# Gated linear attention and an eight-expert layer in one kernel: other places for the expert searches, the weight splits and one table update

## The chip, the cores and the metric

The kernel runs on one core of a Trainium2 chip. The metric is the device time of one launch in microseconds (us); lower is better. Inside the core, TensorE (PE; PEld is its weight load), VectorE (DVE), ScalarE (ACT) and GpSimd (POOL) work side by side, each through its own instructions strictly in the order in which they were written. SyncE (SP) and, for a few transfers, ACT and POOL issue DMAs.

## What is computed

Two stages follow each other. The first is a gated linear recurrence for 4 batches of 8 heads (768 steps, head size 48). The second routes the resulting 3072 rows of 384 numbers to 8 experts, 384 rows each, and applies each expert's two-layer network. Routing is greedy: all (row, expert) scores are taken from the highest down, and a row goes to the first expert that still has room.

```python
for t in range(S):                                   # first stage
    state = alpha[:, :, t, :, None] * state + einsum('bhd,bhe->bhde', k[:, :, t], v[:, :, t])
    y[:, :, t] = einsum('bhd,bhde->bhe', q[:, :, t], state)
x = y.transpose(0, 2, 1, 3).reshape(3072, 384)

order = argsort(-(x @ w_gate).flatten())             # second stage
for idx in order:
    tok, e = idx // 8, idx % 8
    if assigned[tok] >= 0 or counts[e] >= 384: continue
    assigned[tok] = e; counts[e] += 1
for e in range(8):
    out[assigned == e] = relu(x[assigned == e] @ w1[e]) @ w2[e]
```

## The kernel before, in words

**First stage (to about 130 us of the span).** 24 steps of scans, small matmuls and transposes make the rows x, which go to a DRAM tile `x_dram`, and the router's logits `L` (128 partitions x 24 columns x 8 experts). The change doesn't touch it.

**Routing as eight searches.** Instead of sorting, the kernel finds the expert that fills up first, settles its rows, and repeats. Each search compares a 32-bit key in five digits, "levels" 0 to 4:

- `table` (L595, instruction L547): DVE compares every row's digit with all values of a ramp and writes a table `cmp`, 3072 columns wide in levels 0 and 1, 1536 or 1560 in levels 2 to 4.
- `counts` (L598): PE sums the table in 24 small matmuls.
- `reached` (L603): DVE compares the counts with the room left, giving `g` (L605).
- `flags` (L585): one PE matmul spreads `g`, and DVE reduces it to `k` (L588). `next_digit` makes `nd` (L592) and the next level's table follows.

After level 4 come `find` (which expert, and the issue of the first half of its weights' DMAs), `offsets`, `places`, `one_hot` (DVE writes `hot`, 3072 columns, L682, and then `rhs`, L684), `index` (24 PE matmuls over `hot`, L691) and `gather` (DVE turns the result into `idx`, L696; POOL issues three indirect DMAs that fetch the expert's rows `xr`, L698; SP then issues the second half of the weights). `best_left` takes the filled expert out of `L` (L720), finds each row's best remaining logit `m_c` (L721), and makes new digits; `new_choice` and `left` finish that.

**Expert networks on PE.** Each fp32 product is made of three matmuls with split operands: weights as `whi` (ACT copies, `split_hi`, L771 and L772) and `wlo` (POOL subtractions of 128x384, `split_lo`, L780; 16 for an expert, n = 0 to 15, two for each of eight column groups q), rows as `xh` (ACT, L801) and `xl` (DVE, L806). `ffn1` of group q (f1(q), 9 matmuls, L818) leaves `h` in PSUM. ACT makes `hh` of it (L823), then DVE `hl` (L824), and `ffn2` of group q (f2(q), 9 matmuls, L838) uses both. An expert has 144 such product matmuls in the order f1(0), f1(1), f1(2), f2(0), f1(3), f2(1), ... f1(7), f2(5), f2(6), f2(7). `hh` and `hl` of a group are written into their engines' order together with the last matmul of that group.

**What sets the order.** From L956 on a plan gives every step of the searches a position counted in product matmuls: `at(pos, step)` puts a step ahead of product `pos`. The loop at L963 plans round i from a position `base`. Round i starts with `index` results of expert i, fetches expert i's rows, splits its weights, and runs the search for expert i+1, all between products of expert i-1 and the first products of expert i. A round lasts `end` products; `offs` are the positions of the five levels, `hi` and `lo` those of the weight splits, and the triples after `rows` those of the row transposes. Rounds 1 to 5 have a five-level search; round 6 has a short one, round 7 none. What stands ahead of round 1 (round 0) is written out by hand (L921 to L960).

**POOL and DVE.** `BEHIND` (L15) gives for each n which DVE instruction of the running search the POOL subtraction n has to wait for (a dependency made by hand, L780 to L786): entries 0 to 4 are the five tables. For the last expert another rule holds.

Of the kernel before, what the change touches and what calls it, by code (L numbers as in the profile page):

```python
# [11 lines left out]
F16 = mybir.dt.float16  # L12
ROUTE_AHEAD = 3
LAST_BLOCKS = 2
BEHIND = (0, 0, 0, 1, 1, 2, 2, 3, 3, 4, 4, 4, 4, 4, 4, 4)  # L15
FREE_LAST = 4
WARM_UP = 10
Y_IN_LEVEL = (None, 11, 8, 8, 8)
# [8 lines left out]
OP = mybir.AluOpType  # L27
# [3 lines left out]
def gla_moe_kernel(ctx, tc, q, k, v, alpha, w_gate, w1, w2, out):  # L31
    nc = tc.nc
# [9 lines left out]
    E = w_gate.shape[1]  # L42
# [20 lines left out]
    BIGNEG = -3.0e38  # L63
# [455 lines left out]
    def col(x, n=NU):  # L519
        return x[:, None, :].to_broadcast([128, n, x.shape[-1]])  # L520
# [157 lines left out]
    def one_hot(i):  # L678
        hot = st["hot"] = rw.tile([128, NW, T, U], F16, name="hot", bufs=1)
        rhs = st["rhs"] = rw.tile([128, NU, NB], F16, name="rhs")  # L680
        for a, js in enumerate(halves(i)):
            x = nc.vector.tensor_tensor(words(hot, T, js), keyed(st["wb"], T, js), each(iota, T, js), op=OP.is_equal)  # L682
            if a == 0:
                nc.vector.tensor_tensor(rhs, st["bk"], row(cst_c, NB), op=OP.mult)  # L684
        if i == E - 1:
            compared[i] = [None] * FREE_LAST + [x]

    def index(i):
        ix = psx.tile([128, NB], F32, name="xt")
# [27 lines left out]

    def best_left(i):
        es, v = st["es"], st["v"]
        nc.vector.scalar_tensor_tensor(L, col(cl_c), BIGNEG, L, op0=OP.mult, op1=OP.add)  # L720
        nc.vector.tensor_reduce(m_c, L, axis=X, op=OP.max)  # L721
        nc.vector.scalar_tensor_tensor(sel_c, v, float(CAP), qe_c, op0=OP.is_le, op1=OP.mult)
        val = st["val"] = rw.tile([128, NU, E], BF, name="val")
        if i + 2 < E:
            sg = rw.tile([128, NU], I32, name="sg")
            nc.vector.tensor_scalar(sg, m_c.bitcast(I32), 31, -2 ** 31, op0=OP.arith_shift_right,
                                    op1=OP.bitwise_or)
            nc.vector.scalar_tensor_tensor(asg, sel_c, es, asg, op0=OP.mult, op1=OP.add)  # L728
            nc.vector.tensor_tensor(key_c, m_c.bitcast(I32), sg, op=OP.bitwise_xor)
            nc.vector.tensor_tensor(val, L, row(m_c, E), op=OP.is_equal)  # L730
            nc.vector.tensor_tensor(di_c, key_c[:, None, :].to_broadcast([128, nb, NU]), shifts,
                                    op=OP.logical_shift_right)
            nc.vector.tensor_tensor(di_c, di_c, masks, op=OP.bitwise_and)
            top = st["top"] = rw.tile([128, NU], BF, name="top")
            nc.vector.tensor_scalar(top, di_c[:, 0], 1.0, None, op0=OP.add)
            st["d"] = top
        else:
            nc.vector.scalar_tensor_tensor(asg, sel_c, es, asg, op0=OP.mult, op1=OP.add)
            nc.vector.tensor_tensor(val, L, row(m_c, E), op=OP.is_equal)
# [35 lines left out]
    def split_lo(i, n):  # L775
        q, h = divmod(n, 2)
        if (i, q) not in CH:
            return False
        hi, lo, x = CH[i, q]
        y = nc.gpsimd.tensor_sub(lo[:, h], x[h], hi[:, h])  # L780
        if i + 1 in compared:
            after = compared[i + 1][BEHIND[n] if i + 2 < E else min(n, FREE_LAST)]
            if after is not None:
                tc.add_manual_dep(y.ins, after.ins.name,
                                  mybir.DependencyInfo(mybir.DependencyClass.Sync, mybir.DependencyReason.DATA),
                                  reason="weights split while the search reads one table at a time")  # L786
# [96 lines left out]
    def at(pos, fn, *args):  # L883
        plan.append((pos, len(plan), fn, args))
# [76 lines left out]
        at(p, split_lo, 0, n)  # L961
    base = 90
    for i in range(1, E):  # L963
        offs = dict(enumerate((36, 51, 65, 79, 93)))
        end = 140 if i == 1 else 144
        renewed(base, i) if i < E - 1 else at(base, gather, i)
        if i < E - 1:
            at(base + 9, new_choice, i)
        if i < E - 2:
            at(base + 14, table, i + 1, 0)  # L970
            at(base + 14, left, i)
        for b, p in enumerate((25, 34, 41) if i < E - 1 else (45, 60, 75)):
            at(base + p, rows, i, b)
        if i < E - 2:
            levels(base, i + 1, offs, {0: (0, 1), 1: (2,)})
            found(base + offs[4] + 3, i + 1, end - offs[4] - 3)
        else:
            for b, p in enumerate((29, 38, 45) if i < E - 1 else (49, 64, 79)):
                at(base + p, rows_lo, i, b)
        if i == E - 2:  # L980
            at(base + 12, find_last, i + 1)
# [3 lines left out]
            end = 58  # L985
            at(base + end, index, i + 1)
        if i < E - 2:
            hi = (24, 32, 50, 64, 86, 98, 108, 118)
            lo = (26, 26, 32, 55, 55, 71, 71, 87, 87, 103, 103, 103, 108, 108, 118, 118)
        elif i == E - 2:  # L990
            hi = (24, 32, 50, 64, 80, 96, 106, 118)
            lo = (26, 27, 32, 33, 50, 51, 64, 65, 80, 81, 96, 97, 106, 107, 118, 119)
        else:
            hi = [80 + 18 * q for q in range(5)] + [160, 170, 206]
            lo = [x for p in hi for x in (p, p + 1)]
# [70 lines left out]
```

## Time and profile before

| | |
|---|---|
| three timed runs | 425.99, 426.4 (median), 431.81 us |
| the profiled execution | 424.76 us, its span 423.1 us |
| busy share of the span | PE 93%, PEld 82%, DVE 68%, POOL 63%, ACT 46% |
| granted TensorE clock | 0.978 over the span |
| first `index` matmul (L691) of experts 0 to 7 | 151.35, 183.53, 216.58, 250.24, 284.01, 317.76, 351.52, 363.85 us |

Times in the trace are counted from the start of the span. The `index` matmuls make good milestones: round i runs from the i-th of them to the next, so rounds 2 to 5 take 33.7 to 33.8 us each and round 1 takes 33.05 us. A row of the timeline has the start, the duration, the engine, the source line, the operation, what it writes and reads, and in brackets how long the engine sat idle before it and what ended that. In the rows the shown duration of a matmul overlaps with the next one: products start 0.17 us apart, though each is shown with 0.33 us. So a wait of PE is the idle time in brackets plus about 0.17 us.

### The profile page before, as it was taken

How to read it: one execution, taken by the hardware profiler on the slowest of the kernel's cores; microseconds unless marked ns; L12 is line 12 of the kernel's file. 1: busy time of each engine (PE TensorE's matmuls, PEld its weight loads, DVE VectorE, ACT ScalarE, POOL GpSimd, SP SyncE). 2: the span in 40 equal slices, each digit the busy share in tenths (PEclk: the TensorE clock that was granted, in tenths of full speed). 3: DMA queues.
4: the chain of work that ended last, by engine and by line, in shares of the span. 5: the costliest groups of instructions: out<-in, count | busy, mean ns of one | idle time of the engine just before them, and what ended most of it. 6: DMA issues, size and time to landing. Idle time of an engine off the chain costs nothing.

```text
span 423.1 us, 10874 instructions
## 1 busy us (share of the span) xinstructions
PE 394.1 (93%) x4151; PEld 345.5 (82%) x4151; DVE 288.8 (68%) x836; ACT 194.0 (46%) x447; POOL 268.3 (63%) x327
## 2 busy tenths in 40 slices
PE   7999999889898958999999999999999999999993
PEld 3787777677676637998899899899899899999993
DVE  8888787888745686697697688589578677521220
ACT  2477566566575523425325325424343443654511
POOL 4668978677730026646566765665785775799932
PEclk9699999999999989999999999999999999999997
DMA  8999997670004577054055145155153333961011
GB/s 289 320 253 242 243 253 221 179 203 28 2 2 151 196 221 240 21 185 150 4 185 167 58 160 195 39 170 177 66 169 106 139 120 106 338 221 58 5 53 57
DMA packets 34884, 63.40 MB, mean 150 GB/s; under 512 B 3360, under 2 KB 15392, under 8 KB 34832
## 3 DMA queue, kind: packets, MB, share of 16 engines
q1 hardware_dynamic: 28592, 48.54, 37.9%
q0 software_dynamic: 3072, 9.44, 6.9%
q10 hardware_dynamic: 3168, 4.72, 3.2%
q8 instruction: 33, 0.54, 0.5%
q14 instruction: 19, 0.16, 0.1%
HBM read 53.25 MB, written 9.44 MB: 148 GB/s over the span
## 4 chain that ended last, share of the span: by engine, by line
PE 69%; DVE 17%; issue 4%; POOL 3%; ACT 3%; DMA 1%; DVEq 0%; ACTq 0%; POOLq 0%
PE y L838 18%; PE h L818 18%; PE rt L600 6%; PE y L314 5%; PE y L308 5%; PE s L259 5%; DVE hot L682 3%; DVE cmp L547 3%; PE xt L251 3%; POOL wlo L780 2%; PE st L327 2%; PE st L281 2%; DVE sc L222 2%; PE xt L691 2%; DVE ga L227 2%
## 5 line engine op out<-in xcount | busy, mean ns | idle before, releaser
L780 POOL TENSOR_TENSOR wlo<-w1r,whi 128x384 fp32r<-128x384 f32 x64 | 64.9, 1015 | 30.6 <-ACT whi L771 13.7
L823 ACT ACTIVATE hh<-h 128x384 fp32r<-128x384 f32 x64 | 31.5, 492 | 114.8 <-PE h L818 105.9
L780 POOL TENSOR_TENSOR wlo<-w2r,whi 128x384 fp32r<-128x384 f32 x64 | 66.4, 1037 | 20.7 <-DVE cmp L547 13.2
L824 DVE SCALAR_TENSOR_TENSOR hl<-h,hh 128x384 fp32r<-128x384 f32 x64 | 35.4, 553 | 46.8 <-ACT hh L823 45.7
L838 PE MATMUL y<-whi,hl 128*128 128x384 f32 x192 | 66.6, 347 | 0.0
L838 PE MATMUL y<-wlo,hh 128*128 128x384 f32 x192 | 65.8, 342 | 0.0
L838 PE MATMUL y<-whi,hh 128*128 128x384 f32 x192 | 65.3, 340 | 0.0
L698 POOL DMA_INDIRECT xr<-x_dram,idx x24 | 23.2, 966 | 51.4 <-DVE asg L728 29.3
L271 POOL TENSOR_SCALAR_AFFINE_SELECT sm<-sm 128x512 f32<-128x512 f32 x48 | 29.4, 639 | 31.5 <-ACT sm L267 31.5
L818 PE MATMUL h<-xh,whi 128*128 128x384 f32 x192 | 46.8, 344 | 0.4 <-ACT xh L801 0.3
L818 PE MATMUL h<-xh,wlo 128*128 128x384 f32 x192 | 45.8, 345 | 0.0
L818 PE MATMUL h<-xl,whi 128*128 128x384 f32 x192 | 45.8, 340 | 0.0
L292 ACT ACTIVATE sb<-st,sc 128x48 f32<-128x48 f32 x80 | 24.6, 331 | 35.8 <-DVE st L299 21.4
L838 PEld LDWEIGHTS y<-wlo,hh 128*128 128x128 f32 x192 | 36.2, 188 | 0.2
L838 PEld LDWEIGHTS y<-whi,hl 128*128 128x128 f32 x192 | 36.3, 189 | 0.0
L838 PEld LDWEIGHTS y<-whi,hh 128*128 128x128 f32 x192 | 36.1, 188 | 0.0
L771 ACT ACTIVATE whi<-w1r 128x384 fp32r<-128x384 f32 x64 | 33.1, 518 | 6.1 <-DMA w1r<-in_moe_w_dram 6.1
L547 DVE TENSOR_TENSOR cmp<-nd,iota 128x1536 bf16<-128x1536 bf16 (+7 forms) x32 | 34.6, 1092 | 1.0
L818 PEld LDWEIGHTS h<-xh,whi 128*128 128x128 f32 x192 | 33.9, 189 | 1.1 <-ACT xh L801 0.6
L855 POOL DMA_INDIRECT out_dram<-yt,idx x24 | 26.1, 1087 | 12.9 <-ACT yt L842 8.9
L818 PEld LDWEIGHTS h<-xl,whi 128*128 128x128 f32 x192 | 34.0, 188 | 0.0
L600 PEld LDWEIGHTS <-cmp 128*128 128x128 bf16 x720 | 26.3, 118 | 9.4 <-DVE cmp L547 6.6
(183 smaller groups left out, 817.4 us busy)
## 6 DMA issues: line engine op xcount, KB each, us to landing
w1r<-in_moe_w_dram SPq DMA_DIRECT2D x15, 768.0 KB, 4.7
w2r<-in_moe_w_dram SPq DMA_DIRECT2D x15, 768.0 KB, 6.2
vt<-in_v_dram SPq DMA_DIRECT2D x24, 256.0 KB, 6.0
x_dram<-xg ACTq DMA_DIRECT2D x6, 768.0 KB, 3.6
raw_a<-in_alpha_dram SPq DMA_DIRECT2D x19, 226.2 KB, 6.7
raw_k<-in_k_dram SPq DMA_DIRECT2D x19, 224.0 KB, 7.3
raw_q<-in_q_dram SPq DMA_DIRECT2D x19, 224.0 KB, 7.6
raw_a<-in_alpha_dram SPq DMA_DIRECT2D x5, 258.5 KB, 4.3
```

Source lines behind the costliest of these rows:

```text
L271: nc.gpsimd.affine_select(SM[s][:, h], SM[s][:, h], pattern=[[0, 4], [1, C]], compare_op=OP.is_ge, fill=0.0, base=0, channel_multiplier=-1)
L292: nc.scalar.activation(SB[s, u][:, :D], St[p], AF.Copy, scale=ac)
L547: x = nc.vector.tensor_tensor(words(dst, nt, js), keyed(d, nt, js), each(iotas[t], nt, js), op=OP.is_ge)
L600: nc.tensor.matmul(rt[:, 32:40], st["cmp"][:, j // U, :, j % U], st["o"][:, j], start=(j == 0), stop=(j == NU - 1))
L698: got = [nc.gpsimd.indirect_dma_start(out=XR[i][:, b], out_offset=None, in_=x_dram, in_offset=bass.IndirectOffsetOnAxis(ap=IDX[i][:, b:b + ...
L771: nc.scalar.activation(hi[:, 0], a, AF.Copy)
L780: y = nc.gpsimd.tensor_sub(lo[:, h], x[h], hi[:, h])
L818: nc.tensor.matmul(o, a[:, 0, d], x[:, d], start=(n == 0), stop=(n == 3 * DB - 1))
L823: nc.scalar.activation(hh, o, AF.Relu)
L824: nc.vector.scalar_tensor_tensor(hl, o, 0.0, hh, op0=OP.max, op1=OP.subtract)
L838: nc.tensor.matmul(Y[b], a[:, bs], w[:, 1].rearrange("p a b -> p (a b)"), start=(q == 0 and n == 0), stop=(q == FB - 1 and n == 2))
L855: st_ = nc.gpsimd.indirect_dma_start(out=out, out_offset=bass.IndirectOffsetOnAxis(ap=IDX[i][:, b:b + 1], axis=0), in_=yts.pop((i, b)), in ...
```

## The change

1. The levels, the table of level 0, the third row transpose (in rounds 1 to 6) and the end of round 1 get other positions: round 1 ends after 135 products instead of 140, with levels at 36, 51, 63, 76, 89 instead of 36, 51, 65, 79, 93; rounds 2 to 5 have level 1 at 52 instead of 51 and level 0's table at 19 instead of 14. Because round 1 is five products shorter, every later round stands five products earlier against the experts' products.
2. The ACT copies of a weight group (`hi`) and most POOL subtractions (`lo`) are planned sooner, the last two subtractions (n = 14 and 15) later.
3. `one_hot` enters its compare into the list that `BEHIND` refers to, and n = 14 and 15 now wait for it.
4. The update of `L` and the reduction to `m_c` move from `best_left` (behind `idx`) to the end of `one_hot` (ahead of `oh` and `idx`).

```diff
-BEHIND = (0, 0, 0, 1, 1, 2, 2, 3, 3, 4, 4, 4, 4, 4, 4, 4)
+BEHIND = (0, 0, 0, 1, 1, 2, 2, 3, 3, 4, 4, 4, 4, 4, 5, 5)
...
     def one_hot(i):
...
-        if i == E - 1:
-            compared[i] = [None] * FREE_LAST + [x]
+        compared[i] = [None] * FREE_LAST + [x] if i == E - 1 else compared.get(i, []) + [x]
+        if i < E - 1:
+            nc.vector.scalar_tensor_tensor(L, col(cl_c), BIGNEG, L, op0=OP.mult, op1=OP.add)
+            nc.vector.tensor_reduce(m_c, L, axis=X, op=OP.max)
...
     def best_left(i):
         es, v = st["es"], st["v"]
-        nc.vector.scalar_tensor_tensor(L, col(cl_c), BIGNEG, L, op0=OP.mult, op1=OP.add)
-        nc.vector.tensor_reduce(m_c, L, axis=X, op=OP.max)
...
-            after = compared[i + 1][BEHIND[n] if i + 2 < E else min(n, FREE_LAST)]
+            after = compared[i + 1][min(BEHIND[n], len(compared[i + 1]) - 1) if i + 2 < E else min(n, FREE_LAST)]
...
-        offs = dict(enumerate((36, 51, 65, 79, 93)))
-        end = 140 if i == 1 else 144
+        offs = dict(enumerate((36, 51, 63, 76, 89) if i == 1 else (36, 52, 65, 79, 93)))
+        end = 135 if i == 1 else 144
...
-            at(base + 14, table, i + 1, 0)
-            at(base + 14, left, i)
-        for b, p in enumerate((25, 34, 41) if i < E - 1 else (45, 60, 75)):
+            at(base + (14 if i == 1 else 19), table, i + 1, 0)
+            at(base + (14 if i == 1 else 19), left, i)
+        for b, p in enumerate((25, 34, 45) if i < E - 1 else (45, 60, 75)):
...
-            for b, p in enumerate((29, 38, 45) if i < E - 1 else (49, 64, 79)):
+            for b, p in enumerate((29, 38, 49) if i < E - 1 else (49, 64, 79)):
...
         if i < E - 2:
-            hi = (24, 32, 50, 64, 86, 98, 108, 118)
-            lo = (26, 26, 32, 55, 55, 71, 71, 87, 87, 103, 103, 103, 108, 108, 118, 118)
+            hi = (24, 32, 48, 58, 70, 82, 92, 104)
+            lo = (26, 26, 32, 55, 55, 71, 71, 87, 87, 95, 95, 96, 97, 104, 126, 126)
```

The rows below are the order of instructions as built, without times. They are from round 3; rounds 2, 4 and 5 read alike.

**Place 1: PE around level 0's counts.** The rows run from the transpose of the second block of gathered rows (L800) to the first of the 24 matmuls over the table (L600). Before:

```order
L838 MATMUL y_3881<-whi,hl 128x384
L800 MATMUL h<-ident,xr 128x128 x3
L838 MATMUL y_3882<-whi,hh 128x384
L838 MATMUL y_3882<-wlo,hh 128x384
L600 LDWEIGHTS cmp_98
L600 MATMUL rt<-o,cmp_98 128x8
```

Changed:

```order
L818 MATMUL h<-xl,whi 128x384
L800 MATMUL h<-ident,xr 128x128 x3
L818 MATMUL h<-xl,whi 128x384 x2
L600 LDWEIGHTS cmp_98
L600 MATMUL rt<-o,cmp_98 128x8
```

Before, f1(7) (L818) had ended five products ahead of the counts. Now its last product stands directly ahead of them. On DVE the order around this place is the same in both kernels: `hl` of f1(7), two `xl`, then level 0's `g`.

**Place 2: DVE in levels 2 to 4.** The rows run from level 2's `g` to level 4's table (`cmp_98` in the last row). Before:

```order
L605 TENSOR_TENSOR g<-rt,rem 128x8
L824 SCALAR_TENSOR_TENSOR hl<-h,hh 128x384
L588 TENSOR_REDUCE k<-rt 128x1
L592 SCALAR_TENSOR_TENSOR nd<-nd,k,scr 128x24
L547 TENSOR_TENSOR cmp_99<-nd,iota_80 128x6x256
L824 SCALAR_TENSOR_TENSOR hl<-h,hh 128x384
L605 TENSOR_TENSOR g<-rt,rem 128x8
L588 TENSOR_REDUCE k<-rt 128x1
L592 SCALAR_TENSOR_TENSOR nd<-nd,k,scr 128x24
L547 TENSOR_TENSOR cmp_98<-nd,iota_81 128x6x260
```

Changed:

```order
L605 TENSOR_TENSOR g<-rt,rem 128x8
L588 TENSOR_REDUCE k<-rt 128x1
L592 SCALAR_TENSOR_TENSOR nd<-nd,k,scr 128x24
L547 TENSOR_TENSOR cmp_99<-nd,iota_80 128x6x256
L824 SCALAR_TENSOR_TENSOR hl<-h,hh 128x384
L605 TENSOR_TENSOR g<-rt,rem 128x8
L824 SCALAR_TENSOR_TENSOR hl<-h,hh 128x384
L588 TENSOR_REDUCE k<-rt 128x1
L592 SCALAR_TENSOR_TENSOR nd<-nd,k,scr 128x24
L547 TENSOR_TENSOR cmp_98<-nd,iota_81 128x6x260
```

The `hl` that stood between `g` and `k` of level 2 (f1(0)'s) now follows level 3's table, and the next one (f1(1)'s), which followed level 3's table, now stands between `g` and `k` of level 3.

**Place 3: DVE from the last step of `places` to the gather's indices.** Before (`scr` holds, among others, `m_c`):

```order
L675 TENSOR_TENSOR bk<-scr,bsel 128x72
L824 SCALAR_TENSOR_TENSOR hl<-h,hh 128x384
L682 TENSOR_TENSOR hot<-wb,iota 128x3072
L684 TENSOR_TENSOR rhs<-bk,scr 128x72
L824 SCALAR_TENSOR_TENSOR hl<-h,hh 128x384
L711 TENSOR_SCALAR oh<-pcs,k 65x1
L696 TENSOR_SCALAR idx<-xt 128x3
L720 SCALAR_TENSOR_TENSOR L<-scr,L 128x192
L721 TENSOR_REDUCE scr<-L 128x24
```

Changed (from L688 to `best_left` line numbers are two higher):

```order
L675 TENSOR_TENSOR bk<-scr,bsel 128x72
L682 TENSOR_TENSOR hot<-wb,iota 128x3072
L684 TENSOR_TENSOR rhs<-bk,scr 128x72
L687 SCALAR_TENSOR_TENSOR L<-scr,L 128x192
L688 TENSOR_REDUCE scr<-L 128x24
L824 SCALAR_TENSOR_TENSOR hl<-h,hh 128x384 x2
L713 TENSOR_SCALAR oh<-pcs,k 65x1
L698 TENSOR_SCALAR idx<-xt 128x3
```

The `hl` ahead of `hot` (f1(4)'s) has moved behind it, the update of `L` and its reduction stand ahead of `oh` and `idx`, and f1(5)'s `hl` now stands directly ahead of them. POOL's rows have the same order in both kernels in these rounds; what its instructions wait for is what items 2 and 3 change.

## The prediction

> **What bounds the kernel now.** I first read who keeps PE waiting in rounds 1 to 5 (the waits of PE from 180 to 352 us), then how densely products follow each other at the end of the chain that ended last.
>
> ```profile
> PE xt L691 <- DVE rhs L684: 1.9, 5, 0.4
> PE rt L600 <- DVE cmp L547: 1.8, 5, 0.7
> ...
> 386.34 4.68 PE y L838 x27
> ```
>
> PE is the bound: 27 products take 4.68 us, 0.173 us each, so a round's 144 products alone are 25.0 us of its 33.7, and most of the rest is PE's own work for the search. All that PE waits for in the five rounds is on DVE, at two places: `index` waits for `hot` and `rhs` (1.9 us in five waits), `counts` for a table (1.8 us in five). To each wait 0.17 us is added, since the shown end of a product lies that much behind the next possible start. So this change can win some 5 us there, and something in round 0; nothing else in these rounds can be won by moving steps.
>
> The first place, in round 3, on PE, DVE and POOL:
>
> ```profile
> 283.23 0.34 PE L838 MATMUL y<-wlo,hh 128*128 128x384 f32 x1
> 284.01 0.93 PE L691 MATMUL xt<-rhs,hot 128*128 128x3 f16 x24 [0.44 <-DVE rhs L684]
> ...
> 183.53 0.92 PE L691 MATMUL xt<-rhs,hot 128*128 128x3 f16 x24 [0.23 <-DVE rhs L684]
> ...
> 279.26 0.22 DVE L675 TENSOR_TENSOR bk<-scr,bsel 128x72 f16<-128x72 int32 x1
> 280.15 0.56 DVE L824 SCALAR_TENSOR_TENSOR hl<-h,hh 128x384 fp32r<-128x384 f32 x1 [0.67 <-ACT hh L823]
> 280.62 3.19 DVE L682 TENSOR_TENSOR hot<-wb,iota 128x3072 f16<-128x3072 bf16 x1
> 283.74 0.22 DVE L684 TENSOR_TENSOR rhs<-bk,scr 128x72 f16<-128x72 f16 x1
> ...
> 280.23 1.00 POOL L780 TENSOR_TENSOR wlo<-w1r,whi 128x384 fp32r<-128x384 f32 x1
> 281.19 1.00 POOL L780 TENSOR_TENSOR wlo<-w2r,whi 128x384 fp32r<-128x384 f32 x1
> ...
> L682 DVE TENSOR_TENSOR hot<-wb,iota x1: 1747/1747/1747, 181.6 to 181.6; 128x3072 f16<-128x3072 bf16 x1
> ```
>
> `hot` is late twice over: DVE first sits idle for an `hl`, and then `hot` takes 3.19 us where the same instruction at 181.6 us took 1.75. The two POOL subtractions end at 282.19; from there `hot` needs 1.62 us. It stood still while they ran. PE loses 0.44 + 0.17 = 0.61 us. Of the group's 1.9 us, 0.23 fall to the start of round 1 (183.53), whose `hot` wasn't held; the other four share the rest, 0.42 each.
>
> The second place is a level's chain, again in round 3 (level 2's counts, its flags, level 3's counts):
>
> ```profile
> 265.92 0.96 PE L600 MATMUL rt<-o,cmp 128*128 128x8 bf16 x24
> 267.18 0.18 PE L586 MATMUL rt<-g,one 128*128 128x8 bf16 x1
> 269.85 0.96 PE L600 MATMUL rt<-o,cmp 128*128 128x8 bf16 x24 [0.28 <-DVE cmp L547]
> ...
> 267.37 0.49 ACT L823 ACTIVATE hh<-h 128x384 fp32r<-128x384 f32 x1 [1.16 <-PE rt L586]
> ...
> 266.92 0.17 DVE L605 TENSOR_TENSOR g<-rt,rem 128x8 bf16<-128x8 f32 x1 [1.57 <-PE rt L600]
> 267.90 0.56 DVE L824 SCALAR_TENSOR_TENSOR hl<-h,hh 128x384 fp32r<-128x384 f32 x1 [0.81 <-ACT hh L823]
> 268.37 0.15 DVE L588 TENSOR_REDUCE k<-rt 128x1 f32<-128x8 f32 x1
> 268.84 0.96 DVE L547 TENSOR_TENSOR cmp<-nd,iota 128x1536 bf16<-128x1536 bf16 x1
> ```
>
> The flags matmul is done at 267.36, but `k` starts at 268.37: an `hl` stands ahead of it that waits for `hh` (f1(0) has just ended on PE). The table comes a microsecond late, and PE loses 0.28 + 0.17 = 0.45 us.
>
> **The change part by part.** *Hot in rounds 2 to 5.* The `hl` ahead of `hot` is gone, but f1(3)'s now stands ahead of `places`. f1(3) ends on PE 3.6 us after level 4's counts begin, `hh` and `hl` (0.53 later, 0.47 long, as above) end at about 4.7, so `places` is 0.7 us later than before:
>
> ```profile
> 273.33 0.96 PE L600 MATMUL rt<-o,cmp 128*128 128x8 bf16 x24
> ...
> 277.31 0.29 DVE L654 TENSOR_TENSOR_SCAN cum<-ones_c,scr 128x24 f32<-128x24 f32 x2
> ```
>
> Before, `cum` started 3.98 us after the counts and `bk` 1.95 later. So `hot` starts at 4.7 + 2.1 = 6.8, instead of 7.3. Subtractions 9 to 13 are let go by level 4's table, ending about when the counts begin: five at 1.0 us end at 5, ahead of `hot`. 14 and 15 now wait for `hot`. It takes 1.75, `rhs` 0.2: ready at 8.8. PE gets to `index` after 0.8 + 51 x 0.173 + 0.1 = 9.8. The wait goes, with 1.0 us to spare: four times 0.59 (0.42 + 0.17), **-2.4 us**. If copies still blocked it, nothing would be won.
>
> *Flags of level 0, rounds 2 to 5.* This is where I see the price. In round 3 before:
>
> ```profile
> 257.61 0.49 PE L800 MATMUL h<-ident,xr 128*128 128x128 f32 x3
> 258.30 0.97 PE L600 MATMUL rt<-o,cmp 128*128 128x8 bf16 x24
> 259.70 0.17 PE L586 MATMUL rt<-g,one 128*128 128x8 bf16 x1
> ...
> 257.92 0.55 DVE L824 SCALAR_TENSOR_TENSOR hl<-h,hh 128x384 fp32r<-128x384 f32 x1
> 258.38 0.55 DVE L806 TENSOR_TENSOR xl<-xt,xh 128x384 fp32r<-128x384 f32 x1
> 259.02 0.56 DVE L806 TENSOR_TENSOR xl<-h,xh 128x384 fp32r<-128x384 f32 x1
> 259.49 0.15 DVE L605 TENSOR_TENSOR g<-rt,rem 128x8 bf16<-128x8 f32 x1
> ```
>
> The flags came 1.40 us after the counts began; undisturbed they come 1.26 after (265.92 to 267.18, also two products between). DVE's queue is the same in the changed kernel, `hl` of f1(7), two `xl`, then `g`, but f1(7)'s last product now starts 0.17 us before the counts. From the counts' start: its `h` is ready at +0.2. ACT first makes `xh` of the second rows, whose transposes begin at -0.6, so from -0.1, and takes up `hh` about 0.4 later, at +0.3. `hl` follows 0.53 behind, at +0.85; each of `hl`, `xl`, `xl` holds DVE 0.47, so `g` starts at +2.25 and the flags matmul 0.21 later (259.49 to 259.70), at +2.45. PE stands there from +1.26: it loses 1.2 us instead of 0.14. Four rounds: **+4.2 us** (from 0, if DVE somehow came to `g` in time, to 1.7 each, if `hh` came 0.6 later). Behind it nothing is late: level 1's counts come 14 products and a transpose after the flags, 2.9 us, and the table needs 0.7 + 1.75.
>
> *Levels 2 to 4, rounds 2 to 5.* The blocked `k` moves from level 2 to level 3: same neighbours, same 14 products from counts to counts, tables of 1536 and 1560 columns. The 0.45 us stays, at level 4's counts: **0**.
>
> *Round 1.* Its worst wait is level 4's counts:
>
> ```profile
> 205.14 0.15 DVE L588 TENSOR_REDUCE k<-rt 128x1 f32<-128x8 f32 x1
> 207.02 0.96 PE L600 MATMUL rt<-o,cmp 128*128 128x8 bf16 x24 [0.68 <-DVE cmp L547]
> ```
>
> Here too an `hl` stood ahead of `k`. Now f1(2)'s comes behind the table, and 13 products instead of 14 lie between the counts: 0.85 us goes. Two small ones come: f1(0)'s `hl` ahead of level 2's `g` (+0.2), and `hot`, behind f1(4)'s `hl` and with 15 products to `index` instead of 16 (ready at 9.0 after level 4's counts, PE there at 8.9: up to +0.2). **-0.5 us** (0 to -0.85).
>
> *Round 0.* No products cover the chain there:
>
> ```profile
> 152.42 0.16 DVE L696 TENSOR_SCALAR idx<-xt 128x3 int32<-128x3 f32 x1 [0.40 <-PE xt L691]
> 152.50 0.35 DVE L720 SCALAR_TENSOR_TENSOR L<-scr,L 128x192 f32<-128x192 f32 x1
> 153.27 0.19 DVE L722 SCALAR_TENSOR_TENSOR scr<-v,scr 128x24 f32<-128x24 f32 x1
> 157.12 1.75 DVE L547 TENSOR_TENSOR cmp<-top,iota 128x3072 bf16<-128x3072 bf16 x1
> ...
> 157.42 0.52 PE L800 MATMUL xt<-ident,xr 128*128 128x128 f32 x3 [0.38 <-DMA xr<-x_dram,idx]
> 158.93 0.96 PE L600 MATMUL rt<-o,cmp 128*128 128x8 bf16 x24 [0.99 <-DVE cmp L547]
> ...
> 154.01 1.15 POOL L698 DMA_INDIRECT xr<-x_dram,idx  x1 [29.34 <-DVE asg L728]
> ```
>
> The `L` update and its reduction (0.77 us, from 152.50 to 153.27) now run while PE does `index`; `idx` slips by 0.25, so the chain to the table gains 0.5. The gather isn't touched: it started 1.4 us after `idx` before, against 0.3 in round 3, so it waited for something else (the last store to `x_dram`, I think). Its rows came at 157.4, still ahead of the counts. **-0.5 us** (0 to -0.77).
>
> In later rounds that move hides behind products. Earlier ACT copies only fill ACT's idle time; the last two subtractions end about 1 us after `index` begins and the gather's `idx` comes 1.4 after, so POOL is free for it; their group's products come seven microseconds later. From round 6 on the order is the old one, five products earlier, and PE has no wait there: 0.
>
> The sum is -2.4 + 4.2 - 0.5 - 0.5 = **+0.8 us**. Against the profiled span of 423.1 us that is 423.9, and against that execution's 424.76, 425.6. The median of the timed runs lies 1.6 us above that execution, so I put the time at 426.4 + 0.8 = **427.2 us**.
>
> **The rivals.** *Reliefs without the price:* the flags of level 0 aren't held, as when `hl` no longer lies in front of `g` in time. Then -2.4 - 0.5 - 0.5 = -3.4: **423.0 us**. For it: the three waits removed are read off rows, the price is worked out from an order. Against: DVE can't pass the `hl`, and the two `xl` behind it are in the rows. Chance 0.28.
>
> *A table blocked by copies:* level 4's table, already a microsecond late behind f1(1)'s `hl`, meets subtractions 7 and 8, which level 3's table lets go and a scatter on POOL delays. By my count 8 ends 2.4 us after level 3's counts begin and the table starts at 2.9. If POOL is more than 0.5 us later, the table stands for up to 1 us, and PE with it: four times 1.0 on top of the sum, **431.2 us**. For it: before, two copies held `hot` for 1.57 us (280.62 to 282.19). Against: before, the table in the same place (268.84, 0.96) was not held. Chance 0.17. [...]
>
> **How the numbers follow.** The forecast has 0.50, the reliefs alone 0.28, the blocked table 0.17, and 0.05 is for what I don't see. None of the three cases leaves the 2% (8.5 us) that a measurement of this kernel can about tell from no change, so within 2% gets 0.95, faster 0.02, slower 0.03. The likeliest case alone spans 425 to 429 (0 to 1.7 a round at the flags would be -4.2 and +2.6 around it, the ends being unlikely); the range with the others' centres mostly in is 422.8 to 430.2 us.
>
> **What would show it.** In the profile after: `hot` at 1.75 us and no wait of `index` in rounds 2 to 5; the flags (L586) of level 0 some 2.4 us behind their counts, with `hl` ahead of the two `xl`; level 4's counts instead of level 3's waiting 0.3 us for the table; rounds 2 to 5 at about 34.2 us each, round 1 near 31.7 us with five products fewer (0.87 us), and the first `index` of expert 1 about 0.5 us earlier. I am wrong if the flags come within 1.5 us of the counts, or if `hot` still takes over 2 us.

## The result and the profile after

| | before | changed |
|---|---|---|
| timed runs | 425.88 to 431.81, median 426.06 us | 428.21 to 429.87, median 429.75 us |
| ratio of the times, 95% interval | | 1.0077 (1.0061 to 1.0094) |
| the profiled execution, its span | 424.76, 423.1 us | 428.21, 426.5 us |
| up to the first `index` matmul | 151.35 us | 151.66 us |
| round 0 | 32.18 us | 34.27 us |
| round 1 (140 products, then 135) | 32.90 us | 31.22 us |
| rounds 2 to 5 | 33.81, 33.77, 33.75, 33.76 us | 34.16, 34.22, 34.19, 34.19 us |
| from expert 6's first `index` matmul to the end | 71.53 us | 72.60 us |

The kernel became 0.8% slower, 3.7 us by the medians, where 0.8 us was forecast. The profiled executions differ by 3.45 us of span. Round 0 is 2.1 us longer, round 1 0.8 us shorter apart from the 0.87 us of products that left it, rounds 2 to 5 are 1.7 us longer, and 0.3 and 0.2 us lie ahead of them and behind (1.07 us less the same 0.87). Expert 2's milestone of before was read 0.15 us too late ahead of the prediction (its first `index` matmul starts at 216.43 us), so round 1 of before was 32.90 us.

Who keeps PE waiting, first in round 0 (151 to 186 us), then from 184 to 352 us; the columns are the sum of the waits, their number and the longest:

```profile
PE xt L693 <- DVE rhs L684: 3.4, 2, 3.2
PE y L800 <- DMA xr<-x_dram,idx: 1.1, 1, 1.1
PE rt L717 <- DVE oh L713: 0.3, 1, 0.3
```

```profile
PE rt L586 <- DVE g L605: 3.7, 4, 0.9
PE rt L600 <- DVE cmp L547: 1.2, 4, 0.3
PE xt L693 <- DVE rhs L684: 0.2, 1, 0.2
```

From round 1 on this is what was foreseen: four waits of `flags` are new, the four long waits of `index` are gone (0.2 us at the start of round 1 stays), and the counts still wait four times, 0.3 us each. In round 0 a wait for the third block of gathered rows is new, the 1.1 us in the second line; before, PE waited 0.4 us there, for the first block. Two waits for tables, 1.7 us together before, are gone. The 3.2 us in the first line is the same in both kernels.

**Flags of level 0**, round 3, on PE, DVE and ACT:

```profile
259.38 0.97 PE L600 MATMUL rt<-o,cmp 128*128 128x8 bf16 x24
261.75 0.17 PE L586 MATMUL rt<-g,one 128*128 128x8 bf16 x1 [0.94 <-DVE g L605]
...
260.13 0.56 DVE L824 SCALAR_TENSOR_TENSOR hl<-h,hh 128x384 fp32r<-128x384 f32 x1 [1.16 <-ACT hh L823]
260.61 0.55 DVE L806 TENSOR_TENSOR xl<-xt,xh 128x384 fp32r<-128x384 f32 x1
261.07 0.55 DVE L806 TENSOR_TENSOR xl<-h,xh 128x384 fp32r<-128x384 f32 x1
261.54 0.15 DVE L605 TENSOR_TENSOR g<-rt,rem 128x8 bf16<-128x8 f32 x1
...
259.62 0.48 ACT L823 ACTIVATE hh<-h 128x384 fp32r<-128x384 f32 x1
```

Counted from the counts' start: `hh` at 0.24, `hl` at 0.75, `g` at 2.16, the flags at 2.37 us. Forecast were 0.3, 0.85, 2.25 and 2.45. PE stands for 0.94 + 0.17 us.

**Level 3's `k` and level 4's counts**, round 3:

```profile
273.46 0.56 DVE L824 SCALAR_TENSOR_TENSOR hl<-h,hh 128x384 fp32r<-128x384 f32 x1 [0.82 <-ACT hh L823]
273.94 0.16 DVE L588 TENSOR_REDUCE k<-rt 128x1 f32<-128x8 f32 x1
274.41 0.97 DVE L547 TENSOR_TENSOR cmp<-nd,iota 128x1560 bf16<-128x1560 bf16 x1
...
275.43 0.73 PE L600 MATMUL rt<-o,cmp 128*128 128x8 bf16 x17 [0.29 <-DVE cmp L547]
```

The stall of level 3's counts in the kernel before (0.28 us) stands at level 4's now (0.29 us), and the table isn't held: 0.97 us. (The last row has 17 of the 24 matmuls because the stretch asked for ends at 276 us.)

**Hot**, end of round 3:

```profile
285.53 0.96 PE L693 MATMUL xt<-rhs,hot 128*128 128x3 f16 x24
...
282.38 1.75 DVE L682 TENSOR_TENSOR hot<-wb,iota 128x3072 f16<-128x3072 bf16 x1
```

`hot` takes 1.75 us instead of 3.19 and starts 6.95 us after level 4's counts (forecast 6.8), and `index` waits for nothing.

**Round 0** is where the forecast and the trace part. PE, then DVE, then POOL, in the changed kernel (L865 are filler matmuls, whose results no step reads):

```profile
153.47 5.92 PE L865 MATMUL y<-warm 128*128 128x384 bf16 x18
162.58 0.86 PE L800 MATMUL y<-ident,xr 128*128 128x128 f32 x3 [1.10 <-DMA xr<-x_dram,idx]
...
156.80 1.75 DVE L547 TENSOR_TENSOR cmp<-top,iota 128x3072 bf16<-128x3072 bf16 x1
...
157.06 2.32 POOL L700 DMA_INDIRECT xr<-x_dram,idx  x1 [0.30 <-issue]
```

And the third gather and the third block's transposes before:

```profile
156.73 0.95 POOL L698 DMA_INDIRECT xr<-x_dram,idx  x1 [0.31 <-issue]
...
160.59 0.49 PE L800 MATMUL y<-ident,xr 128*128 128x128 f32 x3
```

Before, the table began at 157.12 us, 0.39 us behind the third gather. Now it begins at 156.80 us, 0.26 us ahead of it, and that gather holds POOL for 2.32 us instead of 0.95; it ends 0.83 us after the table does. The rows of the third block are transposed at 162.58 us instead of 160.59. The clock tells more (windows of 3 us from 160 on; the third number from the end is the granted clock, 1.00 is full), before first:

```profile
160.00:163.00 3.00, 2.73 (x18) 1.91 (x16) 2.27 (x5) 1.51 (x3) 2.04 (x3) 1.00 0.99 299
163.00:166.00 3.00, 2.29 (x33) 2.13 (x34) 2.02 (x6) 1.01 (x2) 1.99 (x2) 1.00 0.94 337
```

```profile
160.00:163.00 3.00, 1.90 (x24) 1.34 (x22) 2.21 (x6) 0.74 (x2) 2.31 (x3) 0.94 0.95 321
163.00:166.00 3.00, 3.00 (x11) 2.11 (x9) 1.56 (x2) 1.31 (x3) 1.80 (x2) 0.50 0.75 216
```

After PE had waited for the rows, its clock was halved once more, from 163 to 166 us, where the first products of expert 0 stand. Three suspects were left: the held gather, the `gone` matmul (L717), which now waits 0.34 us because `oh` stands behind the `L` update, and the clock by itself.

### The profile page after: what moved, and what is told of

Its sections match the earlier page's. It is cut to its first block, busy times and chain, and to the rows that moved or that the text cites. A ratio compares the mean times of both kernels' runs of the same rounds, so it can differ in the third digit from the quotient of the medians.

```text
span 426.5 us, 10878 instructions
## 1 busy us (share of the span) xinstructions
PE 396.9 (93%) x4151; PEld 347.2 (81%) x4151; DVE 281.0 (66%) x836; ACT 193.5 (45%) x447; POOL 265.7 (62%) x327
## 4 chain that ended last, share of the span: by engine, by line
PE 70%; DVE 12%; issue 6%; POOL 6%; ACT 3%; DMA 2%; ACTq 0%; DVEq 0%; POOLq 0%
PE h L818 19%; PE y L838 18%; PE y L314 5%; PE s L259 5%; PE rt L600 5%; PE y L308 5%; POOL wlo L780 4%; PE xt L251 3%; PE st L281 2%; PE st L327 2%; POOL out_dram L855 2%; DVE cmp L547 2%; DVE sc L222 1%; ACT yt L322 1%; DVE ga L227 1%
## 5 line engine op out<-in xcount | busy, mean ns | idle before, releaser
L780 POOL TENSOR_TENSOR wlo<-w2r,whi 128x384 fp32r<-128x384 f32 x64 | 64.9, 1014 | 31.4 <-DVE cmp L547 16.9
L838 PE MATMUL y<-whi,hh 128*128 128x384 f32 x192 | 67.5, 351 | 0.0
L838 PE MATMUL y<-whi,hl 128*128 128x384 f32 x192 | 65.6, 342 | 0.0
L700 POOL DMA_INDIRECT xr<-x_dram,idx x24 | 24.5, 1022 | 41.8 <-DVE val L730 29.4
L818 PE MATMUL h<-xh,whi 128*128 128x384 f32 x192 | 47.1, 347 | 0.2 <-DVE hl L824 0.2
L818 PE MATMUL h<-xl,whi 128*128 128x384 f32 x192 | 46.6, 342 | 0.0
L818 PE MATMUL h<-xh,wlo 128*128 128x384 f32 x192 | 45.3, 341 | 0.0
L818 PEld LDWEIGHTS h<-xh,whi 128*128 128x128 f32 x192 | 34.3, 190 | 1.2 <-ACT xh L801 0.6
L818 PEld LDWEIGHTS h<-xh,wlo 128*128 128x128 f32 x192 | 34.6, 190 | 0.0
L818 PEld LDWEIGHTS h<-xl,whi 128*128 128x128 f32 x192 | 33.7, 188 | 0.0
L547 DVE TENSOR_TENSOR cmp<-nd,iota 128x1536 bf16<-128x1536 bf16 (+7 forms) x32 | 32.8, 1035 | 0.9
L772 ACT ACTIVATE whi<-w2r 128x384 fp32r<-128x384 f32 x64 | 33.0, 516 | 0.4 <-DMA w2r<-in_moe_w_dram 0.4
```

Source lines behind the costliest of these rows:

```text
L547: x = nc.vector.tensor_tensor(words(dst, nt, js), keyed(d, nt, js), each(iotas[t], nt, js), op=OP.is_ge)
L700: got = [nc.gpsimd.indirect_dma_start(out=XR[i][:, b], out_offset=None, in_=x_dram, in_offset=bass.IndirectOffsetOnAxis(ap=IDX[i][:, b:b + ...
L772: nc.scalar.activation(hi[:, 1], c, AF.Copy)
L818: nc.tensor.matmul(o, a[:, 0, d], x[:, d], start=(n == 0), stop=(n == 3 * DB - 1))
L838: nc.tensor.matmul(Y[b], a[:, bs], w[:, 1].rearrange("p a b -> p (a b)"), start=(q == 0 and n == 0), stop=(q == FB - 1 and n == 2))
```

## The experiments

Theory 1 says that round 0 is lost because the table of the next search now starts ahead of the third gather on POOL. The rivals are that the clock drops by itself ahead of the gather, or that the `gone` matmul is to blame. For rounds 2 to 5 the theory is that of the prediction: level 0's flags wait because f1(7) ends directly ahead of the counts. Ten kernels were run. The rounds in the table are those of each one's profiled execution, in us. Each ratio is against executions of the kernel before that were timed together with that kernel, so it isn't the quotient of two medians in this document.

| kernel | median us | ratio to before, 95% interval | round 0 | round 1 | rounds 2 to 5 |
|---|---|---|---|---|---|
| changed | 429.75 | 1.0077 (1.0061 to 1.0094) | 34.27 | 31.22 | 34.16 to 34.22 |
| r0_old | 427.13 | 1.0011 (0.9978 to 1.0044) | 32.15 | 31.22 | 34.19 to 34.20 |
| r0_warm | 429.84 | 1.008 (1.005 to 1.011) | 33.94 | 31.23 | 34.18 to 34.21 |
| oh_first | 429.9 | 1.0086 (1.0056 to 1.0117) | 35.78 | 31.21 | 34.17 to 34.21 |
| l_only | 428.12 | 1.005 (1.0023 to 1.0077) | 35.49 | 32.81 | 33.75 to 33.79 |
| copies_only | 423.17 | 0.9938 (0.9902 to 0.9974) | 32.18 | 32.54 | 33.20 to 33.24 |
| phase140 | 426.18 | 0.9987 (0.9958 to 1.0015) | 35.45 | 32.07 | 33.22 to 33.26 |
| phase140_r0 | 423.44 | 0.9956 (0.9932 to 0.998) | 33.12 | 32.07 | 33.22 to 33.25 |
| xl_late | 425.8 | 0.9987 (0.9955 to 1.0018) | 33.09 | 31.21 | 33.27 to 33.29 |
| level2_64 | 422.6 | 0.9937 (0.9901 to 0.9973) | 32.17 | 32.08 | 33.21 to 33.22 |
| early_levels | 423.28 | 0.9929 (0.9885 to 0.9972) | 32.17 | 32.02 | 33.24 to 33.26 |

The time up to round 0 wanders by itself: kernels whose first stage is the same reached the first `index` matmul between 151.35 and 153.80 us. So the rounds are compared one by one, and the medians beside them.

### r0_old: the changed kernel with round 0's table update back in its old place

```diff
-        if i < E - 1:
+        if 0 < i < E - 1:
             nc.vector.scalar_tensor_tensor(L, col(cl_c), BIGNEG, L, op0=OP.mult, op1=OP.add)
             nc.vector.tensor_reduce(m_c, L, axis=X, op=OP.max)
...
     def best_left(i):
+        if i == 0:
+            nc.vector.scalar_tensor_tensor(L, col(cl_c), BIGNEG, L, op0=OP.mult, op1=OP.add)
+            nc.vector.tensor_reduce(m_c, L, axis=X, op=OP.max)
```

> The changed kernel, but in round 0 alone the update of L and its reduction stand behind idx again, as before the change. Theory 1 (round 0 was lost through the earlier table, which meets the third gather on POOL, and through the later gone matmul): round 0 (first index matmul of expert 0 to that of expert 1) goes from 34.3 us back to 32.2, and the time falls by 2.1 to about 1.003 of the kernel before. Rival (round 0 was lost to where the half clock happened to fall, whatever DVE's order): round 0 stays near 34.

Round 0 is 32.15 us. The third gather and the table stand as before the change:

```profile
156.93 0.95 POOL L700 DMA_INDIRECT xr<-x_dram,idx  x1 [0.30 <-issue]
...
157.29 1.75 DVE L547 TENSOR_TENSOR cmp<-top,iota 128x3072 bf16<-128x3072 bf16 x1
```

The gather, 0.36 us ahead of the table, takes 0.95 us, and the table 1.75: with the gather first neither is held. All of round 0's loss hangs on the `L` update standing ahead of `idx` in that one round.

### l_only: the kernel before with the table update moved, and nothing else

```diff
     def one_hot(i):
...
+        if i < E - 1:
+            nc.vector.scalar_tensor_tensor(L, col(cl_c), BIGNEG, L, op0=OP.mult, op1=OP.add)
+            nc.vector.tensor_reduce(m_c, L, axis=X, op=OP.max)
...
     def best_left(i):
-        nc.vector.scalar_tensor_tensor(L, col(cl_c), BIGNEG, L, op0=OP.mult, op1=OP.add)
-        nc.vector.tensor_reduce(m_c, L, axis=X, op=OP.max)
```

> The kernel before with one part of the change alone: the update of L and its reduction stand at the end of the one-hot, ahead of oh and idx, in all rounds. Theory (that part is what round 0 lost, and it does nothing later): in round 0 the table starts ahead of the third gather, that gather takes 2.3 us instead of 0.95, round 0 takes 34 us or more, rounds 1 to 5 stay within 0.1 us of before, and the time is 1.005 of the kernel before. Rival (round 0 was lost through something else in the change): round 0 stays at 32.2 us or below and the ratio at 1.000 or below.

Round 0 is 35.49 us, rounds 2 to 5 are what they were before. Table (DVE), gather (POOL) and the wait of PE:

```profile
157.64 1.75 DVE L547 TENSOR_TENSOR cmp<-top,iota 128x3072 bf16<-128x3072 bf16 x1
...
157.89 2.32 POOL L701 DMA_INDIRECT xr<-x_dram,idx  x1 [0.30 <-issue]
...
163.83 0.55 PE L801 MATMUL y<-ident,xr 128*128 128x128 f32 x3 [2.57 <-DMA xr<-x_dram,idx]
```

The move costs 3.3 us in round 0 in this execution, 2.1 us by the medians (428.12 to 426.06), and brings nothing in any later round beyond 0.1 us in round 1.

### oh_first: the changed kernel with `oh` ahead of the update in round 0

```diff
+        if i == 0:
+            take_places(0)
         if i < E - 1:
             nc.vector.scalar_tensor_tensor(L, col(cl_c), BIGNEG, L, op0=OP.mult, op1=OP.add)
...
     index(0)
-    take_places(0)
     gone()
```

> The changed kernel, but in round 0 oh stands ahead of the update of L, so that the gone matmul on PE doesn't come late; the table stays early. Theory 1 (the early table holds the third gather on POOL): that gather still takes 2.3 us or more, PE still waits for its rows, and round 0 takes 33.5 us or more; the time stays near 1.008 of the kernel before. Rival (PE's short idle at the gone matmul keeps the clock at half for a second stretch, and that is what round 0 lost): the half clock lasts 3.4 us, round 0 goes back to 32.2 us, and the time to 1.003.

Round 0 is 35.78 us, with the third gather at 157.65 us (2.37 long) behind the table at 157.45, though `gone` no longer waits. The `gone` matmul isn't the cause.

### r0_warm: the changed kernel with more filler matmuls ahead of round 0's index

```diff
     one_hot(0)
+    spin_more(15)
     index(0)
```

> The changed kernel with 15 filler matmuls on PE ahead of expert 0's index, in the 3.3 us in which PE waits there, so that PE isn't idle. Theory 1 (the gather that meets the table): the granted clock stays full through round 0, but the third block of rows still comes at about 162 us, PE still waits for it, and round 0 takes 33.3 us or more. Rival (the half clock): with the clock full, round 0 takes 32 us or less, and the time falls to about 1.002 of the kernel before.

The fillers themselves came late (they waited for a copy on ACT), so the kernel isn't the clean test it was meant to be. But the clock was full from 151.2 to 164.9 us, over the gathers and their rows, and the round still took 33.94 us. Here the second gather met the table, and PE waited twice, 2.49 and 1.25 us:

```profile
162.14 0.52 PE L800 MATMUL xt<-ident,xr 128*128 128x128 f32 x3 [2.49 <-DMA xr<-x_dram,idx]
...
160.09 1.75 DVE L547 TENSOR_TENSOR cmp<-top,iota 128x3072 bf16<-128x3072 bf16 x1
...
160.19 2.47 POOL L700 DMA_INDIRECT xr<-x_dram,idx  x1 [0.30 <-issue]
```

It was 0.10 us behind the table and took 2.47 us. A full clock over the gathers removes neither the hold nor the waits. It doesn't separate the hold from the later clock: behind the waits, from 164.9 to 168.3 us, the clock was at half here too.

### copies_only: the kernel before with items 2 and 3 of the change alone

```diff
-BEHIND = (0, 0, 0, 1, 1, 2, 2, 3, 3, 4, 4, 4, 4, 4, 4, 4)
+BEHIND = (0, 0, 0, 1, 1, 2, 2, 3, 3, 4, 4, 4, 4, 4, 5, 5)
...
-            hi = (24, 32, 50, 64, 86, 98, 108, 118)
-            lo = (26, 26, 32, 55, 55, 71, 71, 87, 87, 103, 103, 103, 108, 108, 118, 118)
+            hi = (24, 32, 48, 58, 70, 82, 92, 104)
+            lo = (26, 26, 32, 55, 55, 71, 71, 87, 87, 95, 95, 96, 97, 104, 126, 126)
```

(with `one_hot`'s compare in the list and the `min`, as in the change)

> The kernel before with one part of the change alone: weight copies sooner and the last two subtractions behind hot. Theory (hot was late because copies held it): hot takes 1.75 us in rounds 2 to 5, index waits no more there, each of these rounds loses 0.59 us, to 33.15, and the time falls by 2.4 us, to 0.994 of the kernel before. Rival (hot was late because of the hl ahead of it): hot still ends too late, rounds 2 to 5 keep 33.5 us or more.

Rounds 2 to 5 fall from 33.77 to 33.22 us, and round 1 by 0.36 us. `index` waits only at the start of round 1, 0.2 us. The one `hl` ahead of `hot` (first line) is still there, at its old place:

```profile
280.00 0.56 DVE L823 SCALAR_TENSOR_TENSOR hl<-h,hh 128x384 fp32r<-128x384 f32 x1 [0.66 <-ACT hh L822]
280.47 1.75 DVE L682 TENSOR_TENSOR hot<-wb,iota 128x3072 f16<-128x3072 bf16 x1
```

The whole of the relief at `index` comes from items 2 and 3, which keep POOL's subtractions out of `hot`'s way (`hot` takes 1.75 us instead of 3.19; neither item was tried without the other). It needs no other position of any level, and this version takes 0.6% less than the kernel before (0.9902 to 0.9974 of it), where the whole change takes 0.8% more.

### phase140: the changed kernel with round 1's old length

```diff
-        end = 135 if i == 1 else 144
+        end = 140 if i == 1 else 144
```

> The changed kernel, but round 1 lasts 140 products again, so that the later rounds stand as before against the products. Theory (flags of level 0 wait for g because f1(7) ends directly ahead of the counts): that wait goes back to 0.14 us, hot still ends in time, rounds 2 to 5 take 33.1 to 33.2 us instead of 34.2, and the time falls by about 4 us against the changed kernel, to 0.998 of the kernel before. Rival (the wait at the flags came from the new place of level 0's table at 19): the wait stays at 1.1 to 1.2 us and rounds 2 to 5 at 34.2.

Who keeps PE waiting from 184 to 352 us:

```profile
PE rt L600 <- DVE cmp L547: 1.1, 4, 0.3
...
```

The waits of `flags` are gone, and rounds 2 to 5 take 33.24 us instead of 34.19: 0.95 us in each is the price of standing five products earlier against the experts. The time is level with before because round 0 still has the held gather (35.45 us here).

### phase140_r0: both repairs together

```diff
-        if i < E - 1:
+        if 0 < i < E - 1:
...
-        end = 135 if i == 1 else 144
+        end = 140 if i == 1 else 144
```

> The changed kernel with both losses undone: round 1 lasts 140 products again, and in round 0 the update of L stands behind idx as before the change. Theory: the parts add up. Round 0 takes 32.2 us, round 1 32.1 (no wait at level 4's counts), rounds 2 to 5 33.2 each, and the time is 0.993 of the kernel before, 3 us less. Rival (the gains are tied to the new phase or to the earlier update): one of these rounds is longer by 0.5 us or more, and the ratio is 0.996 or more.

423.44 us, 0.9956 of before. In the profiled execution the first gather came 3.8 us after `index` began instead of 2.7, and so the third one met the table although the order was the old one: it started 0.73 us behind the table and took 1.83 us, round 0 33.12 us. That round was expected at 32.2 us, and the ratio at 0.993; the other rounds came as expected. The hold thus comes with the meeting and not with the order as such. The old order doesn't forbid the meeting, though the other five kernels with it escaped.

### xl_late: the changed kernel with the two `xl` behind level 1's table

```diff
-            levels(base, i + 1, offs, {0: (0, 1), 1: (2,)})
+            levels(base, i + 1, offs, {0: (0, 1), 1: (2,)} if i == 1 else {1: (2,)})
+            if i > 1:
+                for b in (0, 1):
+                    at(base + 38, rows_lo, i, b)
```

> The changed kernel, but in rounds 2 to 5 the two xl of the first rows stand behind level 1's table instead of ahead of level 0's g, so that only the hl of f1(7) is ahead of it. Theory (each of the three holds DVE for 0.47 us): the flags of level 0 come 1.5 us after the counts instead of 2.5, PE waits 0.3 us instead of 1.2, rounds 2 to 5 take 33.3 us, and the time falls by 3 to 4 us against the changed kernel. Rival (the wait is for hh on ACT or for xh, not for DVE's own work): the flags come 2.2 us or more after the counts and the rounds stay at 34.

Rounds 2 to 5 take 33.28 us: with the two `xl` (0.47 us each) out of `g`'s way the flags don't wait, at the changed kernel's own positions. In round 3 they come 1.43 us after the counts, which start at 257.99 us:

```profile
259.42 0.17 PE L586 MATMUL rt<-g,one 128*128 128x8 bf16 x1
```

So the `hl` alone wasn't the price; it was the three instructions in a row.

This execution also separates the gather from the clock in round 0, where it has the changed kernel's instructions. Its clock in windows of 4 us:

```profile
156.00:160.00 4.00, 4.00 (x15) 2.09 (x14) 3.08 (x8) 1.35 (x3) 3.39 (x3) 0.53 0.37 98
160.00:164.00 4.00, 2.69 (x39) 1.97 (x37) 2.63 (x6) 1.04 (x3) 2.98 (x4) 1.00 0.77 248
164.00:168.00 4.00, 3.75 (x41) 3.20 (x40) 2.07 (x6) 1.75 (x4) 1.99 (x2) 1.00 0.84 273
```

The third gather takes 2.32 us here too and PE waits 1.31 us for its rows, but the clock stays full afterwards: 33.09 us. Such windows of copies_only, whose gather isn't held:

```profile
152.00:156.00 4.00, 3.89 (x35) 2.54 (x36) 3.33 (x15) 0.52 (x1) 1.15 (x1) 0.50 0.82 257
156.00:160.00 4.00, 3.19 (x23) 1.83 (x22) 3.83 (x11) 1.84 (x4) 2.03 (x3) 0.80 0.52 145
```

There, too, the clock was at half for all of the first window and low in the second, and the round took 32.18 us, no more than r0_old's with a shorter such stretch.

### level2_64: phase140_r0 with level 2 one product sooner

```diff
-        offs = dict(enumerate((36, 51, 63, 76, 89) if i == 1 else (36, 52, 65, 79, 93)))
+        offs = dict(enumerate((36, 51, 63, 76, 89) if i == 1 else (36, 52, 64, 79, 93)))
```

> As the previous kernel of this call (round 1 with 140 products, the old order in round 0), and level 2 of rounds 2 to 5 one product sooner, at 64 instead of 65, so that its flags and the next table are written ahead of the hl of f1(0). Theory (a table comes late where an hl stands between g and k): the waits of counts for a table in rounds 2 to 5 go, 0.45 us each, the rounds take 32.8 us, and the time is 0.989 of the kernel before. Rival (the table is late for another reason, such as copies on POOL): the waits stay, at this or another level, and the rounds at 33.2.

422.6 us, but rounds 2 to 5 stay at 33.22 us; the expected 32.8 missed. The counts no longer wait; f1(2) does. In round 3, the last products of f1(1) and the first of f1(2):

```profile
267.88 0.69 PE L821 MATMUL h<-xl,whi 128*128 128x384 f32 x3
268.71 0.79 PE L821 MATMUL h<-xh,whi 128*128 128x384 f32 x3
```

The third of the first three starts about 268.23 us, and the next product 0.48 us behind it instead of 0.17. The `hl` that now stands behind level 3's table is late, and it is what frees the buffer that f1(2) writes (from the order; not tested by itself). The wait moved: 0.31 us here, where it had been 0.45.

### early_levels: phase140_r0 with all five levels sooner

```diff
-        offs = dict(enumerate((36, 51, 63, 76, 89) if i == 1 else (36, 52, 65, 79, 93)))
+        offs = dict(enumerate((36, 51, 63, 76, 89) if i == 1 else (34, 49, 61, 73, 87)))
...
-            at(base + (14 if i == 1 else 19), table, i + 1, 0)
+            at(base + 14, table, i + 1, 0)
...
-            levels(base, i + 1, offs, {0: (0, 1), 1: (2,)})
+            levels(base, i + 1, offs, {0: (0, 1) if i == 1 else (0,), 1: (2,)})
+            if i > 1:
+                at(base + offs[0] + 2, rows_lo, i, 1)
```

> As the kernel with round 1 at 140 products and the old order in round 0, but in rounds 2 to 5 the levels stand at 34, 49, 61, 73, 87 (level 0's table at 14), so that every hl of f1 comes behind a table or behind the counts, with time left before its h buffer is needed; the xl of the second rows stands behind level 1's table. Theory (the 0.45 us a round that is left is the hl of f1(0) in a bad place, ahead of k or too late for f1(2)): no wait of 0.3 us or more is left in rounds 2 to 5, they take 32.8 us, and the time is 0.989 of the kernel before. Rival (a search's chain of five levels is as long as the room that the products give it, so the wait turns up at another level): the rounds stay at 33.1 us or more.

Rounds 2 to 5 stay at 33.25 us. The wait came back at other levels, as the rival said, but by a road that neither named. Round 3, DVE, POOL, and level 3's counts on PE:

```profile
263.84 0.96 DVE L547 TENSOR_TENSOR cmp<-nd,iota 128x1536 bf16<-128x1536 bf16 x1
266.98 1.53 DVE L547 TENSOR_TENSOR cmp<-nd,iota 128x1536 bf16<-128x1536 bf16 x1
...
263.91 1.77 POOL L858 DMA_INDIRECT out_dram<-yt,idx  x1 [0.16 <-issue]
...
266.68 1.01 POOL L783 TENSOR_TENSOR wlo<-w1r,whi 128x384 fp32r<-128x384 f32 x1
...
268.57 0.96 PE L600 MATMUL rt<-o,cmp 128*128 128x8 bf16 x24 [0.25 <-DVE cmp L547]
```

The scatter of finished rows starts 0.07 us behind level 2's table and takes 1.77 us; the two subtractions behind it on POOL come late; the second is in flight when level 3's table is due, and the table takes 1.53 us instead of 0.96. This is the blocked table that the prediction held for a rival, and it is set off by the same meeting of table and indirect DMA as in round 0. Whether the levels could stand sooner with other places for the subtractions wasn't tried.

## Why the prediction was right in most steps and wrong in one

The median of 429.75 us lies inside the stated range, but 2.5 us above the forecast and beyond the 429 us given for the likeliest case: 3.7 us were lost where 0.8 were forecast. That the range holds it is luck. The range reached so far because of the blocked table (431.2 us), which didn't happen; what filled the room was a loss in round 0 that no rival had.

**Hot, rounds 2 to 5: right.** Forecast -2.4 us; copies_only has the relief alone, 33.77 to 33.22 us, four times 0.55, -2.2 us. The changed places of the `hl` that the prediction counted through were not needed for it.

**Flags of level 0: right.** Forecast +4.2 us; changed kernel against phase140, 34.19 to 33.24 us, four times 0.95, +3.8 us. The chain `hh`, `hl`, `xl`, `xl`, `g` is in the rows as forecast, 0.1 us sooner.

**Levels 2 to 4: right.** The stall of 0.45 us (0.28 and the 0.17) moved to level 4's counts, 0.46 us. Rounds 2 to 5 came out at 34.2 us, as said.

**Round 1: right in kind, -0.8 instead of -0.5 us.** The wait of level 4's counts, 0.68 us, is gone. The two small losses that were set against it (0.2 us at level 2's `g`, up to 0.2 at `hot`) didn't come; in copies_only 0.36 us of the gain is there with the earlier copies alone.

**From round 6 on: right** within 0.2 us.

**Round 0: the step that failed.** Forecast -0.5 us, measured +2.1. The prediction said that the chain to the table gains 0.5 us and "The gather isn't touched". The table did start sooner, 5.14 us after the first `index` matmul instead of 5.77, and the third gather where it had stood, at 5.40 instead of 5.38. But so DVE began ahead of the third gather, by 0.26 us where it had been 0.39 us behind, and the gather was held. Its row (156.73 us) and the table's (157.12 us) were both in the trace; I looked at what the gather waited for and at when its first rows came, and not at what runs beside it while POOL works on it. The cost runs through three steps:

- The hold: all six kernels with the earlier table show it in their profiled execution, 2.32 us instead of 0.95 in three (changed, l_only, xl_late), 2.29 and 2.37 in two (phase140, oh_first), and 2.47 at the second gather in r0_warm. Of the six with the old order one does, phase140_r0.
- The rows come about 2 us later, and PE, which had the third block in time before, waits for them: 1.1 to 2.6 us.
- In four of those executions (changed, l_only, oh_first, phase140) the clock then drops a second time, and in r0_warm it drops there for the first time in the round. In xl_late it doesn't drop.

From one profiled execution each, the hold by itself is worth 33.09 - 32.17 = 0.9 us (xl_late against level2_64; phase140_r0, held in part, agrees with 33.12); these are the two held rounds without a later drop of the clock. The later drop of the clock comes on top. Three kernels have the same instructions in round 0: xl_late without a later drop (33.09 us), the changed kernel with 3.4 us of half clock (34.27) and phase140 with 6.8 us (35.45). That makes 1.2 and 2.4 us more; of the 2.4, 0.2 is that the third block's rows came later. Three of expert 0's first products in the changed kernel, then in xl_late:

```profile
164.02 1.33 PE L818 MATMUL h<-xh,whi 128*128 128x384 f32 x3
...
164.48 0.79 PE L818 MATMUL h<-xh,whi 128*128 128x384 f32 x3 [0.26 <-ACT xh L801]
```

Why the clock drops in some executions of the same instructions and not in others wasn't settled. The later stretches of half clock last 3.4 us (changed) and 6.8 us (l_only, oh_first, phase140), and xl_late and the changed kernel have the same instructions in round 0 and differ in it. No run shows what causes a drop.

The forecast gain was there at the table and didn't reach PE in the changed kernel's profiled execution. The fillers ahead of level 0's counts ran at half clock and took 5.92 us (4.37 before), and the counts began 7.89 us after the first `index` matmul instead of 7.58. In l_only they began at 6.95, 0.6 us sooner as the prediction had it, and the wait for the third block's rows came after that.

That the trace of before held the warning shows in a scatter there, against one of the changed kernel. Before first, then the change, table on DVE, scatter on POOL:

```profile
264.39 0.96 DVE L547 TENSOR_TENSOR cmp<-nd,iota 128x1536 bf16<-128x1536 bf16 x1
264.68 1.55 POOL L855 DMA_INDIRECT out_dram<-yt,idx  x1 [0.16 <-issue]
```

```profile
266.50 1.01 POOL L855 DMA_INDIRECT out_dram<-yt,idx  x1 [0.16 <-issue]
266.63 0.96 DVE L547 TENSOR_TENSOR cmp<-nd,iota 128x1536 bf16<-128x1536 bf16 x1
```

Behind the table's start the scatter takes 1.55 us, ahead of it 1.01, and the table takes 0.96 either way. The prediction read off that subtractions in flight hold `hot` (3.19 us instead of 1.75) and didn't ask the same of the indirect DMAs.

The sum, against the span: +0.3 (before round 0), +2.1, -0.8, +1.7, +0.2 make 3.5 of the 3.45 us; forecast were 0, -0.5, -0.5, +1.8 and 0. Of the rivals, the reliefs without the price is what phase140_r0 comes near (423.44 us, forecast 423.0), by another position and not by DVE passing the `hl`; but 0.5 us of that forecast was a gain in round 0, which no run brought. The blocked table stayed away from the changed kernel: none of its tables in rounds 1 to 5 is held (0.96 to 0.97 us, and 1.75 to 1.76 in levels 0 and 1).

## What to carry to other kernels

Before making a step on DVE sooner, list what POOL has in flight at the new time, its DMA issues as much as its arithmetic: a start that moved by 0.6 us past another cost 2.1 us here. When a change has several parts, ask which part alone brings the gain: here the new places and waits of the weight splits bring nearly all that was won (423.17 us; the new levels of round 1 add about 0.5 us in phase140_r0), while the shift of later rounds by five products and the earlier update of `L` cost 3.8 and 2.1 us. And a wait that was removed should be looked for at the next step in line (level2_64, early_levels) before it is booked as won.

## What the runs showed of the hardware that I had not expected

- An indirect DMA issued by POOL behind the start of one of the searches' tables (the DVE compare at L547) is held. In the traces of the kernel before and the changed one, and in rows of the other ten (round 0, and parts of round 3 in three), 15 such DMAs started 0.07 to 1.06 us behind a table's start; they took 1.51 to 2.47 us and ended 0.81 to 0.89 us after the table. 21 others were already under way when a table started, for 0.02 to 0.85 us; they took 0.95 to 1.02 us, and none of these tables was slower for it (0.96 to 0.97 and 1.75 us). One pair in level2_64 started at the same time to 0.01 us (271.30 us), and neither was held (0.99 and 1.00 us). No run moved the table alone, so this rests on the order of starts in the traces.
- Half the clock in front of the gathered rows cost nothing in round 0 of copies_only (32.18 us with 5.5 us of it, 32.15 in r0_old with 3.4), while 3.4 us of it behind them cost about 1.2 us in the changed kernel, where it lay over expert 0's first products.
